# Gated window attention at decode: z turned by VectorE in column quarters, y and the gate among the queries, and wo's first piece loaded in two halves around the last values

## The chip, the cores and the metric

The kernel runs on one core of one Trainium2 chip. A time is the device time of one execution in microseconds; of several executions of a kernel the median is given. The profile is that of one further execution, taken by the hardware profiler; times inside it are counted from the start of its span. PE is TensorE's matrix array, PEld its weight load, DVE VectorE, ACT ScalarE, POOL GpSimd and SP SyncE, whose queue issues the large loads here.

## What is computed

One token for each of two sequences passes a layer norm, an attention over the last W = 4096 positions of a cache (32 query heads, 8 key and value heads, head size 128), and beside it a gated MLP; the attention's output is multiplied by silu of the MLP's output and added to x. All is float32.

```python
W = min(4096, max(256, Sk // 4))
xn = _layernorm(x)
q = (xn @ wq) as [B, 32, 1, 128]
k, v = k_cache[:, :, Sk - W:, :], v_cache[:, :, Sk - W:, :]   # repeated for 4 query heads each
p = softmax(q . k * 128 ** -0.5)
s = (p @ v) as [B, 1, 4096] @ wo                              # [4096, 512]
z = _gelu(xn @ w_in)                                          # [512, 1792]
z1, z2 = z[..., :896], _layernorm(z[..., 896:])
g = silu((z1 * (w_sp * z2 + b_sp)) @ w_out)                   # [896, 512]
out = x + s * g
```

The keys and values that are read are 2 x 8 x 4096 x 128 floats each, 33.6 MB; wq and wo are 8.4 MB each, w_in 3.7 MB and w_out 1.8 MB: 89.4 MB in all for a few matrix-vector products.

## The kernel before

**Loads.** Everything large is issued on SP's queue, in the order of the program. A ring of four buffers of 4 MB (`slot`, 32 KB in each of the 128 partitions) receives first w_in and the two halves of wq, then the keys and values, and last wo. The attention is done in eight units of two key and value heads of one sequence; `K:u` and `V:u` load the 4 MB of keys and the 4 MB of values of unit u. A load into a buffer waits, on SP, until the last reader of what was in it is done, and the loads behind it wait too.

**A unit.** VectorE turns the keys of a unit in eight pieces of 32 x 32 blocks (`T:u.q`), TensorE multiplies them with the queries in two halves (`shares`, `scores`, with a copy by ScalarE, `keep`, between), VectorE takes the maximum (`rowmax`, `mg`, `bias`), ScalarE the exponentials (`exp`), VectorE turns the probabilities (`probs_t`), TensorE multiplies them with the values in two halves (`pv:u.0`, `pv:u.1`), ScalarE scales the result (`evac`) and TensorE and VectorE collect it (`col`, `gather`). Units 0 to 3 belong to the first sequence, 4 to 7 to the second.

**wo.** The attention's 4096 outputs per sequence are split into three sets (`SETS`): set 0 from the units 0, 1, 4 and 5, set 1 from 2 and 6, set 2 from 3 and 7. `spread:i` and `oT:i` bring set i into the form of weights. `wo:0` loads the 4 MB of wo that belong to set 0 and `wo:1` the 2 MB of set 1 and the 2 MB of set 2, the latter in pieces of 4, 2, 1 and 1 blocks (a block is 256 KB). `X`, `Y` and `U` are the multiplications of set 0, of set 1 and of the first four blocks of set 2, two blocks in a step, accumulated over the four 32-column strips of the array in `part`; `parts:0` copies `part` to SBUF, `pz:0` sums its four strips into `so`, and `Z:n` adds the last three pieces of set 2 to `so`, in steps of one column quarter for each strip. Two operations of VectorE and a store to `out` end the program.

**Order.** All engines but POOL run in program order. From `K:0` on, that order is the text `ORDER` (lines 27 to 52), read from left to right; before that it is the order of the code. The change touches the code of lines 236 to 354 (the MLP and the queries), the text of `ORDER`, and the functions `load_wo`, `wo_early`, `wo_last` and `add_parts` (lines 518 to 563).

**The front part.** `z` (lines 236 to 248) multiplies xn with w_in, one bank for each quarter of the columns, with the four parts of the sum over 512 left apart in the four strips; the copy to SBUF is followed by 14 multiplications of z with a selection of rows (`zT_ps`), which sum the strips and turn the result. The gelu, the layer norm and `hT` follow on VectorE, with `queries(0)` to `queries(3)` (q = xn wq, one for each quarter of the sum) put between them on TensorE; then come `y` (hT w_out), the placing of the queries (`qs`, `qx`, `xm`, `qa`, `place_queries`) and `y_sum`; the gate is computed by the step `silu:0` in unit 0's work.

Each line of the trace is put down to line 65, the helper `InOrder`, so the tiles' names tell the operations apart.

Of the kernel before, what the change touches and what calls it, by code (L numbers as in the profile page):

```python
# [24 lines left out]


ORDER = """
K:0 K:1 V:0 T:0.0 q:0 T:0.1 T:0.2 T:0.3 shares:0.0 T:0.4 T:0.5 T:0.6 keep:0.0 scores:0.0 T:0.7 shares:0.1 keep:0.1
scores:0.1 rowmax:0.0
K:2 V:1 T:1.0 T:1.1 T:1.2 rowmax:0.1 mg:0 shmax:0 T:1.3 silu:0 bias:0 shares:1.0 T:1.4 exp:0.0 probs_t:0.0 T:1.5 T:1.6  # L30
exp:0.1 keep:1.0 pv:0.0 lsum:0 shsum:0 scores:1.0 T:1.7 shares:1.1 probs_t:0.1 pv:0.1 weights:0 keep:1.1 scores:1.1
evac:0 col:0 rowmax:1.0
K:3 V:2 T:2.0 T:2.1 T:2.2 rowmax:1.1 mg:1 shmax:1 T:2.3 bias:1 shares:2.0 T:2.4 exp:1.0 probs_t:1.0 T:2.5 T:2.6 exp:1.1
# [10 lines left out]
scores:5.1 evac:4 col:4 rowmax:5.0  # L44
K:7 V:6 T:6.0 rowmax:5.1 mg:5 T:6.1 T:6.2 shmax:5 bias:5 T:6.3 exp:5.0 T:6.4 exp:5.1 T:6.5 probs_t:5.0 shares:6.0
keep:6.0 lsum:5 shsum:5 scores:6.0 probs_t:5.1 T:6.6 T:6.7 rowmax:6.0 pv:5.0 weights:5 shares:6.1 keep:6.1 pv:5.1
V:7 T:7.0 wo:0 scores:6.1 rowmax:6.1 T:7.1 T:7.2 mg:6 T:7.3 shmax:6 bias:6 T:7.4 evac:5 col:5 exp:6.0 exp:6.1 T:7.5
probs_t:6.0 T:7.6 T:7.7 wo:1 lsum:6 shares:7.0 keep:7.0 pv:6.0 scores:7.0 shares:7.1 rowmax:7.0 keep:7.1 shsum:6
scores:7.1 probs_t:6.1 weights:6 rowmax:7.1 mg:7 pv:6.1 evac:6 shmax:7 gather:5 col:6 bias:7 exp:7.0 gather:6 exp:7.1
probs_t:7.0 spread:0 probs_t:7.1 lsum:7 spread:1 pv:7.0 shsum:7 oT:0 weights:7 pv:7.1 X:0.6 X:0.0 oT:1 X:0.2 X:0.4  # L50
evac:7 X:0.3 col:7 X:0.7 gather:7 spread:2 X:0.5 Y:0.1 Y:0.0 Y:0.3 X:0.1 Y:0.2 oT:2 U:0.0 U:0.1 parts:0 Z:0 pz:0 Z:1 Z:2
"""


# [16 lines left out]
def kernel(  # L71
# [14 lines left out]
    pe, dve, act, sp = (InOrder(tc, e) for e in (nc.tensor, nc.vector, nc.scalar, nc.sync))  # L86
    B, _, D = x.shape
# [39 lines left out]
    for a in range(0, KT, 2):  # L127
        t = slot(f"wq{a}", 2, HQ * DH)
# [30 lines left out]
    xnT = cst.tile([P, KT, 32], F32, tag="xnT", name="xnT")  # L159
# [3 lines left out]
    hT = cst.tile([P, FT, 32], F32, tag="hT", name="hT")  # L163
# [6 lines left out]
    rowm = cst.tile([P, 32], F32, tag="rowm", name="rowm")  # L170
# [24 lines left out]
    pt = bank("xnT_ps", KT, B)  # L195
# [30 lines left out]
    for nj in (8, 16):  # L226
# [3 lines left out]
        at = cst.tile([P, nx], F32, tag=f"at{nj}", name=f"at{nj}")  # L230
# [2 lines left out]

    assert KT == G
    z = kts.tile([P, F], F32, tag="kts", name="z")
    for n in range(G):
        pz = bank(f"z{n}", 512)[:, :FC]
        for k in range(KT):  # L240
            pe.matmul(
                pz[32 * k : 32 * k + 32, :], xnT[:, k, :], win[:, k, n * FC : (n + 1) * FC],
                start=True, stop=True,
            )
        if n % 2:
            dve.tensor_copy(z[:, n * FC : (n + 1) * FC], pz)
        else:
            act.activation(z[:, n * FC : (n + 1) * FC], pz, AF.Copy)
    wb_ps = ps.tile([P, 512], F32, tag="mo", name="wb_ps")[:, :2]
    pe.matmul(wb_ps, ones[0:1, :], wb1, start=True, stop=True)  # L250
    wb = cst.tile([P, 2], F32, tag="wb", name="wb")
    dve.tensor_copy(wb, wb_ps)
    pt = bank("zT_ps", 2, FT, B)
    zv = z.rearrange("b (h p j) -> b h j p", h=2, j=FT)
    for h in range(2):
        for j in range(FT):
            pe.matmul(pt[:, h, j, :], zv[:, h, j, :], rowm[:, :B], start=True, stop=True)


    assert HKV == NR * G  # L260
    pq = [ps.tile([P, 512], F32, tag=f"s{r}", name=f"q_ps{r}") for r in range(NR)]
# [1 line left out]
    def queries(k):  # L263
        for r in range(NR):
            for g in range(G):
                c = (r * G + g) * 512
                pe.matmul(
                    pq[r][32 * g : 32 * g + 32, :], xnT[:, k, :], wqt[k][:, c : c + 512],
                    start=(k == 0), stop=(k == KT - 1),
                )  # L270

    queries(0)
    zT = cst.tile([P, 2, FT, B], F32, tag="zT", name="zT")
    dve.tensor_copy(zT, pt)
    u = cst.tile([P, 2, FT, B], F32, tag="u", name="u")
# [17 lines left out]

    per_b = [[0, FT], [1, B]]
    mean_over_rows(mean, z2, "mean_ps")
    queries(1)
    dve.tensor_scalar_mul(mean, mean, 1.0 / FH)
    dve.tensor_sub(z2, z2, free_ap(mean, 0, per_b))
    dve.tensor_mul(w2, z2, z2)
# [3 lines left out]
    dve.tensor_mul(z2, z2, free_ap(mean, 0, per_b))  # L303
    dve.tensor_scalar(z2, z2, wb[:, 0:1], wb[:, 1:2], op0=ALU.mult, op1=ALU.add)
    dve.tensor_mul(hT[:, :, 0 : 16 * B : 16], z1, z2)
    queries(2)
    queries(3)

    HC = REP * G
    y = bank("y", D)
    for j in range(FT):
        g = j % G
        pe.matmul(y[32 * g : 32 * g + 32, :], hT[:, j, :], wout[:, j, :], start=(j < G), stop=(j >= FT - G))
    qs = kts.tile([P, NR, 512], F32, tag="kts", name="qs")
    qx = kts.tile([P, NR, HC, 32], F32, tag="kts", name="qx")
    for r in range(NR):
# [3 lines left out]
    for b in range(B):  # L322
# [1 line left out]
            xm[:, b], free_ap(qx, b, [[32 * HC, NR], [0, G], [32, HC]]), free_ap(grpm, 0, [[0, NR], [1, G], [0, HC]]),  # L324
            op=ALU.mult,
        )
    yp = sb.tile([P, D], F32, tag="o", name="yp", bufs=1)
    act.activation(yp, y, AF.Copy)
    qa = bank("qa", NP, G, REP)
    pe.matmul(  # L330
        qa.rearrange("p n c i -> p (n c i)"), same.rearrange("p g c -> p (g c)"),
        xm.rearrange("p b r g (i c) -> p (b r g) c i", c=G), start=True, stop=True,
    )

    y = bank("y_sum", DC)
    for g in range(G):
        pe.matmul(y[32 * g : 32 * g + 32, :], rowm, yp[:, g * DC : (g + 1) * DC], start=True, stop=True)
    ys = cst.tile([P, DC], F32, tag="ys", name="ys")
    act.activation(ys, y, AF.Copy)
# [7 lines left out]
    gate = cst.tile([P, DC], F32, tag="gate", name="gate")

    def silu():
        dve.tensor_scalar(gate, ys, -1.0, 80.0, op0=ALU.mult, op1=ALU.min)  # L350
        act.activation(gate, gate, AF.Exp)
        dve.tensor_scalar_add(gate, gate, 1.0)
        dve.reciprocal(gate, gate)
        dve.tensor_mul(gate, gate, ys)

# [9 lines left out]
    sets = {}  # L365
# [105 lines left out]
    col = {}  # L471
# [43 lines left out]
        wo_s.append(wo[r0:r1, :].rearrange("(p j) d -> p j d", j=nj))  # L515
    blocks = []

    def load_wo(n):
        t = slot(f"wo{n}", 16, D)
        a = 0  # L520
        for i in ((0,), (1, 2))[n]:
            for j, n in (((0, 16),), ((0, 8),), ((0, 4), (4, 2), (6, 1), (7, 1)))[i]:
                sp.dma_start(t[:, a : a + n, :], wo_s[i][:, j : j + n, :])
                blocks.append((t[:, a : a + n, :], sets[f"oT{i}"][1], j))
                a += n

    EARLY = 28
    done = 0
# [1 line left out]
    def wo_early(n, at):  # L530
        nonlocal done
        if done == 0:
            part.append(ps.tile([P, 512], F32, tag="s0", name="part"))
        t, oT, j = blocks[n]
        for a in range(at, at + 2):
            g = done % G
            pe.matmul(
                part[0][32 * g : 32 * g + 32, :], oT[:, j + a, :], t[:, a, :], start=(done < G), stop=(done >= EARLY - G)
            )
            done += 1  # L540
# [5 lines left out]
        act.activation(parts[0], part[0], AF.Copy)  # L546

    def wo_last(n):
        if n == 0:
            so.append(bank("so", DC))  # L550
        t, oT, j = blocks[3 + n]
        for a in range(t.shape[1]):
            for g in range(G):
                pe.matmul(
                    so[0][32 * g : 32 * g + 32, :], oT[:, j + a, :], t[:, a, g * DC : (g + 1) * DC],
                    start=(n == 0 and a == 0), stop=(j + a == oT.shape[1] - 1),
                )

    def add_parts():
        for g in range(G):  # L560
            pe.matmul(
                so[0][32 * g : 32 * g + 32, :], rowm, parts[0][:, g * DC : (g + 1) * DC], start=False, stop=False
            )

    parts, so = [], []
# [79 lines left out]
```

## Time and profile before

| | |
|---|---|
| median of 3 executions | 217.01 us (216.76, 217.04, 217.01) |
| the profiled execution's own time | 217.29 us |
| its span | 215.5 us |
| mean granted TensorE clock | 0.825 |
| busy: PE, DVE, ACT, POOL | 143.2, 126.7, 51.6, 4.5 us |
| read from HBM | 89.40 MB, 415 GB/s over the span |

The profiled execution spends 217.29 - 215.5 = 1.79 us outside the span, and is 0.28 us above the median. A busy time is the sum over an engine's instructions, with overlapping ones counted once; it says nothing of what the end waits for. In the lists of instructions a row gives the start, the duration, the engine, the operation with the tiles that it writes and reads, how many instructions are put together, and in brackets the idle time of the engine before them with what ended it. In the rows of windows the number behind an engine's name is its busy time in that stretch, and the last three are the granted clock of TensorE, the busy share of the DMA engines, and the data rate.

### The profile page before, as it was taken

The numbers are of one execution on the slowest core, as the hardware profiler recorded it, in microseconds if no ns is written. First come the engines' busy times: TensorE is split into PE (matmuls) and PEld (weight loads), VectorE is DVE, ScalarE is ACT, GpSimd is POOL, SyncE is SP. The second block draws the span as 40 slices with busy tenths as digits, with TensorE's granted clock in tenths as the row PEclk, the third lists the DMA queues.
The fourth block names the chain that finished last, engine by engine and source line by source line (L and its number), as shares of the span: only waits on it lengthen the run. The fifth ranks groups of instructions, "written<-read, shape, count | busy, mean of one in ns | idle before, by whom it ended". The sixth has DMA issues, their size and how long they took to land.

```text
span 215.5 us, 2332 instructions
## 1 busy us (share of the span) xinstructions
PE 143.2 (66%) x900; PEld 48.1 (22%) x900; DVE 126.7 (59%) x218; ACT 51.6 (24%) x129; POOL 4.5 (2%) x17
## 2 busy tenths in 40 slices
PE   0179796833854966964991795389259917987793
PEld 0117622111120221222220231123112201232231
DVE  2611213169899799649928972993698099636011
ACT  5011103300116036033330602142051206142201
POOL 8000000000000000000000000000000000000000
PEclk9999569665998896796697599669755997996999
DMA  7999999999999999999999999999999999999990
GB/s 246 432 443 444 398 429 465 414 458 414 456 408 447 420 426 444 426 443 426 450 420 450 408 441 420 426 450 426 447 415 456 401 456 414 447 426 417 420 374 22
DMA packets 3930, 89.54 MB, mean 416 GB/s; under 512 B 446, under 2 KB 462, under 8 KB 848
## 3 DMA queue, kind: packets, MB, share of 16 engines
q1 hardware_dynamic: 3900, 89.40, 96.8%
q8 instruction: 7, 0.11, 0.2%
q14 instruction: 3, 0.02, 0.0%
q10 hardware_dynamic: 20, 0.01, 0.0%
HBM read 89.40 MB, written 0.00 MB: 415 GB/s over the span
## 4 chain that ended last, share of the span: by engine, by line
DMA 63%; PE 23%; DVE 8%; ACT 3%; issue 1%; ACTq 0%
DMA v<-in_A_v_cache_dram 42%; DMA k<-in_A_k_cache_dram 16%; PE acc L65 10%; DMA win<-in_B_w_in_dram 5%; PE sh L65 5%; DVE kts L65 4%; PE part L65 4%; PE s L65 3%; DVE pT L65 1%; ACT p L65 1%; ACT o L65 1%; DVE gate L65 1%; PE mo L65 1%; ACT ss L65 1%; DVE qb L65 1%
## 5 line engine op out<-in xcount | busy, mean ns | idle before, releaser
L65 DVE STREAM_TRANSPOSE kts<-k 128x1024 f32<-128x1024 f32 x64 | 75.6, 1218 | 29.5 <-DMA k<-in_A_k_cache_dram 29.5
L65 PE MATMUL sh<-kts,qb 128*32 128x512 f32 x256 | 41.6, 775 | 13.2 <-DVE kts L65 9.3
L65 PE MATMUL acc<-v,pT 128*32 128x512 f32 x256 | 37.4, 707 | 8.8 <-DVE pT L65 4.4
L65 ACT ACTIVATE p<-s,nb 128x512 f32<-128x512 f32 x32 | 22.5, 733 | 36.2 <-DVE nb L65 36.2
L65 ACT ACTIVATE ss<-sh 128x512 f32<-128x512 f32 x16 | 9.6, 599 | 59.1 <-PE sh L65 59.1
L65 DVE STREAM_TRANSPOSE pT<-p 128x1024 f32<-128x1024 f32 x16 | 19.6, 1225 | 2.3 <-ACT p L65 2.1
L65 PE MATMUL s<-ss,sums 128*128 128x512 f32 x32 | 18.8, 671 | 2.3 <-ACT ss L65 2.3
L65 PE MATMUL mo<-mg,joint 128*128 128x16 f32 x16 | 4.0, 327 | 23.4 <-DVE mg L65 23.4
L65 PEld LDWEIGHTS acc<-v,pT 128*32 128x32 f32 x256 | 10.5, 145 | 35.1 <-issue 27.0
L65 PEld LDWEIGHTS sh<-kts,qb 128*32 128x32 f32 x256 | 8.8, 126 | 34.2 <-issue 28.8
L65 DVE TENSOR_REDUCE m<-s 128x1 f32<-128x512 f32 x16 | 10.7, 671 | 4.2 <-PE s L65 4.2
L65 PE MATMUL q_ps<-wq,xnT 128*32 128x512 f32 x64 | 10.5, 784 | 3.5 <-DMA wq<-in_A_wq_dram 3.5
L65 ACT ACTIVATE o<-acc,wd 128x128 f32<-128x128 f32 x32 | 9.1, 368 | 15.0 <-PE acc L65 15.0
L65 PEld LDWEIGHTS mo<-mg,joint 128*128 128x128 f32 x16 | 3.2, 250 | 27.2 <-DVE mg L65 24.4
L65 PE MATMUL z<-win,xnT 128*32 128x448 f32 x32 | 5.6, 869 | 4.7 <-DMA win<-in_B_w_in_dram 4.7
L65 PE MATMUL part<-wo,oT 128*32 128x512 f32 x56 | 7.7, 596 | 1.4 <-ACT o L65 1.4
L65 PEld LDWEIGHTS s<-ss,sums 128*128 128x128 f32 x32 | 5.0, 197 | 10.3 <-issue 7.7
L65 PE MATMUL zT_ps<-rowm,z 128*128 128x2 f32 x28 | 6.6, 370 | 0.0
L65 PEld LDWEIGHTS zT_ps<-rowm,z 128*128 128x128 f32 x28 | 6.5, 325 | 0.0
L65 ACT ACTIVATION_READ_ACCUMULATOR p<-s,nb 128x1 f32 x32 | 6.5, 203 | 0.0
L65 ACT ACT_TABLE_LOAD x4 | 5.1, 1283 | 2.6 <-POOL hT L164 2.6
L65 DVE COPY z<-z 128x448 f32<-128x448 f32 x2 | 1.3, 626 | 7.5 <-PE z L65 7.5
(111 smaller groups left out, 68.4 us busy)
## 6 DMA issues: line engine op xcount, KB each, us to landing
k<-in_A_k_cache_dram SPq DMA_DIRECT2D x8, 4096.0 KB, 27.4
v<-in_A_v_cache_dram SPq DMA_DIRECT2D x8, 4096.0 KB, 29.8
wq<-in_A_wq_dram SPq DMA_DIRECT2D x1, 4096.0 KB, 24.5
wq<-in_A_wq_dram SPq DMA_DIRECT2D x2, 2048.0 KB
wo<-in_A_wo_dram SPq DMA_DIRECT2D x1, 4096.0 KB, 30.4
win<-in_B_w_in_dram SPq DMA_DIRECT2D x1, 3584.0 KB, 11.5
wo<-in_A_wo_dram SPq DMA_DIRECT2D x1, 2048.0 KB
wout<-in_B_w_out_dram SPq DMA_DIRECT2D x1, 1792.0 KB, 15.3
```

What stands on the lines that cost most here:

```text
L65: return self.tc.keep_in_program_order(call(*args, **kwargs))
```

## The change

z now goes into one bank: the strip g of the array holds the g-th quarter of the columns of both halves of z, and the four parts of the sum are added up in the bank. One copy by ScalarE and one 32 x 32 turn by VectorE give z in the form in which the gelu needs it; the 14 multiplications `zT_ps` are gone. `queries(0)` and `queries(1)` come behind the whole layer norm, then `y`, `queries(2)`, `y_sum` with the gate, and `queries(3)`. The step `silu:0` is gone and `q:0` stands before `T:0.0`.

wo's set 0 is loaded in two halves, `wo:0.0` before `V:7` and `wo:0.1` behind it. The first half takes the ring's buffer of K:6 and V:7 that of V:5, where before V:7 took that of K:6 and wo that of V:5. Set 1 is `wo:1.0`, set 2 comes in pieces of 4, 3 and 1 blocks (`wo:2.0` to `wo:2.2`). The steps on the first half (`X:0.0` to `X:0.3`) stand between the probabilities of unit 7, those on the second half (`X:1.0` to `X:1.3`) behind `pv:7.1`, around `col:7` and `spread:2`; `Y`, `U`, `parts:0` follow, then `pz:0`, `Z:0` and `Z:1`, where before `Z:0` stood ahead of `pz:0`. `part` takes a buffer of `acc` in place of `s0`.

```diff
-K:0 K:1 V:0 T:0.0 q:0 T:0.1 T:0.2 T:0.3 shares:0.0 T:0.4 T:0.5 T:0.6 keep:0.0 scores:0.0 T:0.7 shares:0.1 keep:0.1
+K:0 K:1 V:0 q:0 T:0.0 T:0.1 T:0.2 T:0.3 shares:0.0 T:0.4 T:0.5 T:0.6 keep:0.0 scores:0.0 T:0.7 shares:0.1 keep:0.1
...
-V:7 T:7.0 wo:0 scores:6.1 rowmax:6.1 T:7.1 T:7.2 mg:6 T:7.3 shmax:6 bias:6 T:7.4 evac:5 col:5 exp:6.0 exp:6.1 T:7.5
-probs_t:6.0 T:7.6 T:7.7 wo:1 lsum:6 shares:7.0 keep:7.0 pv:6.0 scores:7.0 shares:7.1 rowmax:7.0 keep:7.1 shsum:6
-scores:7.1 probs_t:6.1 weights:6 rowmax:7.1 mg:7 pv:6.1 evac:6 shmax:7 gather:5 col:6 bias:7 exp:7.0 gather:6 exp:7.1
-probs_t:7.0 spread:0 probs_t:7.1 lsum:7 spread:1 pv:7.0 shsum:7 oT:0 weights:7 pv:7.1 X:0.6 X:0.0 oT:1 X:0.2 X:0.4
-evac:7 X:0.3 col:7 X:0.7 gather:7 spread:2 X:0.5 Y:0.1 Y:0.0 Y:0.3 X:0.1 Y:0.2 oT:2 U:0.0 U:0.1 parts:0 Z:0 pz:0 Z:1 Z:2
+wo:0.0 V:7 wo:0.1 T:7.0 scores:6.1 rowmax:6.1 T:7.1 T:7.2 mg:6 T:7.3 shmax:6 bias:6 T:7.4 evac:5 col:5 exp:6.0 exp:6.1
+T:7.5 gather:5 probs_t:6.0 T:7.6 T:7.7 wo:1.0 wo:2.0 wo:2.1 wo:2.2 lsum:6 shares:7.0 keep:7.0 spread:0 pv:6.0 scores:7.0
+shares:7.1 rowmax:7.0 keep:7.1 shsum:6 oT:0 scores:7.1 probs_t:6.1 weights:6 rowmax:7.1 mg:7 pv:6.1 evac:6 shmax:7 col:6
+bias:7 exp:7.0 gather:6 X:0.0 X:0.1 exp:7.1 probs_t:7.0 X:0.2 X:0.3 probs_t:7.1 lsum:7 spread:1 pv:7.0 shsum:7 weights:7
+pv:7.1 oT:1 X:1.0 evac:7 X:1.1 col:7 X:1.2 gather:7 spread:2 X:1.3 oT:2 Y:0.0 Y:0.1 Y:0.2 Y:0.3 U:0.0 U:0.1 parts:0 pz:0
+Z:0 Z:1
...
-    z = kts.tile([P, F], F32, tag="kts", name="z")
-    for n in range(G):
-        pz = bank(f"z{n}", 512)[:, :FC]
-        for k in range(KT):
+    pz = bank("z", 2, FH // G)
+    for k in range(KT):
+        for g in range(G):
             pe.matmul(
-                pz[32 * k : 32 * k + 32, :], xnT[:, k, :], win[:, k, n * FC : (n + 1) * FC],
-                start=True, stop=True,
+                pz[32 * g : 32 * g + 32], xnT[:, k, :],
+                win[:, k].rearrange("p (h g c) -> p h g c", h=2, g=G)[:, :, g, :],
+                start=(k == 0), stop=(k == KT - 1),
             )
...
+    zs = kts.tile([P, 2, 2, FT, 32], F32, tag="kts", name="zs")
+    act.activation(zs[:, 0], pz.rearrange("p h (i j) -> p h j i", j=FT), AF.Copy)
+    dve.transpose(zs[:, 1].rearrange("p h j i -> p (h j i)"), zs[:, 0].rearrange("p h j i -> p (h j i)"))
+    pt = zs[:, 1, :, :, :B]
...
-    pt = bank("zT_ps", 2, FT, B)
-    zv = z.rearrange("b (h p j) -> b h j p", h=2, j=FT)
-    for h in range(2):
-        for j in range(FT):
-            pe.matmul(pt[:, h, j, :], zv[:, h, j, :], rowm[:, :B], start=True, stop=True)
...
     dve.tensor_mul(hT[:, :, 0 : 16 * B : 16], z1, z2)
-    queries(2)
-    queries(3)
...
+    queries(0)
+    queries(1)
     y = bank("y", D)
...
+    yp = sb.tile([P, D], F32, tag="o", name="yp", bufs=1)
+    act.activation(yp, y, AF.Copy)
+    queries(2)
+    y = bank("y_sum", DC)
...
+    act.activation(gate, gate, AF.Exp)
+    dve.tensor_scalar_add(gate, gate, 1.0)
+    dve.reciprocal(gate, gate)
+    dve.tensor_mul(gate, gate, ys)
+    queries(3)
...
-    def load_wo(n):
-        t = slot(f"wo{n}", 16, D)
-        a = 0
-        for i in ((0,), (1, 2))[n]:
-            for j, n in (((0, 16),), ((0, 8),), ((0, 4), (4, 2), (6, 1), (7, 1)))[i]:
-                sp.dma_start(t[:, a : a + n, :], wo_s[i][:, j : j + n, :])
...
+    PIECES = (((0, 8), (8, 8)), ((0, 8),), ((0, 4), (4, 3), (7, 1)))
+    wo_t = {}
+
+    def load_wo(i, n):
+        if i < 2 and n == 0:
+            wo_t[i] = slot(f"wo{i}", 16, D)
+        t, at = (wo_t[i], 0) if i < 2 else (wo_t[1], 8)
+        j, count = PIECES[i][n]
+        sp.dma_start(t[:, at + j : at + j + count, :], wo_s[i][:, j : j + count, :])
...
-            part.append(ps.tile([P, 512], F32, tag="s0", name="part"))
+            part.append(ps.tile([P, 512], F32, tag="acc", name="part", bufs=2))
...
     def wo_last(n):
-        if n == 0:
-            so.append(bank("so", DC))
-        t, oT, j = blocks[3 + n]
+        t, oT, j = blocks[4 + n]
...
-                    start=(n == 0 and a == 0), stop=(j + a == oT.shape[1] - 1),
+                    start=False, stop=(j + a == oT.shape[1] - 1),
...
     def add_parts():
+        so.append(bank("so", DC))
         for g in range(G):
             pe.matmul(
-                so[0][32 * g : 32 * g + 32, :], rowm, parts[0][:, g * DC : (g + 1) * DC], start=False, stop=False
+                so[0][32 * g : 32 * g + 32, :], rowm, parts[0][:, g * DC : (g + 1) * DC], start=True, stop=False
             )
```

More of the change, by code (lines that the diff above doesn't have):

```diff
@@ L27 @@
 ORDER = """
-K:0 K:1 V:0 T:0.0 q:0 T:0.1 T:0.2 T:0.3 shares:0.0 T:0.4 T:0.5 T:0.6 keep:0.0 scores:0.0 T:0.7 shares:0.1 keep:0.1
+K:0 K:1 V:0 q:0 T:0.0 T:0.1 T:0.2 T:0.3 shares:0.0 T:0.4 T:0.5 T:0.6 keep:0.0 scores:0.0 T:0.7 shares:0.1 keep:0.1
 scores:0.1 rowmax:0.0
-K:2 V:1 T:1.0 T:1.1 T:1.2 rowmax:0.1 mg:0 shmax:0 T:1.3 silu:0 bias:0 shares:1.0 T:1.4 exp:0.0 probs_t:0.0 T:1.5 T:1.6
+K:2 V:1 T:1.0 T:1.1 T:1.2 rowmax:0.1 mg:0 shmax:0 T:1.3 bias:0 shares:1.0 T:1.4 exp:0.0 probs_t:0.0 T:1.5 T:1.6
 exp:0.1 keep:1.0 pv:0.0 lsum:0 shsum:0 scores:1.0 T:1.7 shares:1.1 probs_t:0.1 pv:0.1 weights:0 keep:1.1 scores:1.1
@@ L232 @@
         perms[nj] = to, at
-    assert KT == G
-    z = kts.tile([P, F], F32, tag="kts", name="z")
-    for n in range(G):
-        pz = bank(f"z{n}", 512)[:, :FC]
-        for k in range(KT):
+    assert KT == G and FT * 32 == FH // G
+    pz = bank("z", 2, FH // G)
+    for k in range(KT):
+        for g in range(G):
             pe.matmul(
-                pz[32 * k : 32 * k + 32, :], xnT[:, k, :], win[:, k, n * FC : (n + 1) * FC],
-                start=True, stop=True,
-            )
[L245 to L248, printed above, removed]
+                pz[32 * g : 32 * g + 32], xnT[:, k, :],
+                win[:, k].rearrange("p (h g c) -> p h g c", h=2, g=G)[:, :, g, :],
+                start=(k == 0), stop=(k == KT - 1),
+            )
+    zs = kts.tile([P, 2, 2, FT, 32], F32, tag="kts", name="zs")
+    act.activation(zs[:, 0], pz.rearrange("p h (i j) -> p h j i", j=FT), AF.Copy)
+    dve.transpose(zs[:, 1].rearrange("p h j i -> p (h j i)"), zs[:, 0].rearrange("p h j i -> p (h j i)"))
+    pt = zs[:, 1, :, :, :B]
     wb_ps = ps.tile([P, 512], F32, tag="mo", name="wb_ps")[:, :2]
@@ L270, in queries @@
                 )
-    queries(0)
     zT = cst.tile([P, 2, FT, B], F32, tag="zT", name="zT")
@@ L295 @@
     mean_over_rows(mean, z2, "mean_ps")
-    queries(1)
     dve.tensor_scalar_mul(mean, mean, 1.0 / FH)
@@ L305 @@
     dve.tensor_mul(hT[:, :, 0 : 16 * B : 16], z1, z2)
-    queries(2)
-    queries(3)
-    HC = REP * G
+    queries(0)
+    queries(1)
     y = bank("y", D)
@@ L315 @@
         pe.matmul(y[32 * g : 32 * g + 32, :], hT[:, j, :], wout[:, j, :], start=(j < G), stop=(j >= FT - G))
+    yp = sb.tile([P, D], F32, tag="o", name="yp", bufs=1)
+    act.activation(yp, y, AF.Copy)
+    queries(2)
+    y = bank("y_sum", DC)
+    for g in range(G):
+        pe.matmul(y[32 * g : 32 * g + 32, :], rowm, yp[:, g * DC : (g + 1) * DC], start=True, stop=True)
+    ys = cst.tile([P, DC], F32, tag="ys", name="ys")
+    act.activation(ys, y, AF.Copy)
+    gate = cst.tile([P, DC], F32, tag="gate", name="gate")
+    dve.tensor_scalar(gate, ys, -1.0, 80.0, op0=ALU.mult, op1=ALU.min)
+    act.activation(gate, gate, AF.Exp)
[3 more added lines that the diff above has]
+    queries(3)
+    HC = REP * G
     qs = kts.tile([P, NR, 512], F32, tag="kts", name="qs")
@@ L326 @@
         )
-    yp = sb.tile([P, D], F32, tag="o", name="yp", bufs=1)
-    act.activation(yp, y, AF.Copy)
     qa = bank("qa", NP, G, REP)
@@ L333 @@
     )
[L335 to L339, printed above, removed]
     def place_queries():
@@ L345, in place_queries @@
         )
[L347 to L354, printed above, removed]
     JH = UJ // 2
@@ L516 @@
     blocks = []
-    def load_wo(n):
-        t = slot(f"wo{n}", 16, D)
-        a = 0
-        for i in ((0,), (1, 2))[n]:
-            for j, n in (((0, 16),), ((0, 8),), ((0, 4), (4, 2), (6, 1), (7, 1)))[i]:
-                sp.dma_start(t[:, a : a + n, :], wo_s[i][:, j : j + n, :])
-                blocks.append((t[:, a : a + n, :], sets[f"oT{i}"][1], j))
-                a += n
+    PIECES = (((0, 8), (8, 8)), ((0, 8),), ((0, 4), (4, 3), (7, 1)))
[6 more added lines that the diff above has]
+        sp.dma_start(t[:, at + j : at + j + count, :], wo_s[i][:, j : j + count, :])
+        blocks.append((t[:, at + j : at + j + count, :], sets[f"oT{i}"][1], j))
     EARLY = 28
@@ L574, in step @@
             place_queries()
-        elif name == "silu":
-            silu()
         elif name == "K":
@@ L581, in step @@
         elif name == "wo":
-            load_wo(u)
+            load_wo(u, a[0])
         elif name == "spread":
@@ L587, in step @@
         elif name == "X":
-            wo_early(0, 2 * a[0])
+            wo_early(u, 2 * a[0])
         elif name == "Y":
-            wo_early(1, 2 * a[0])
+            wo_early(2, 2 * a[0])
         elif name == "U":
-            wo_early(2, 2 * a[0])
+            wo_early(3, 2 * a[0])
         elif name == "Z":
```

## The prediction

> **What bounds the kernel now.** I read the page first, for the busy shares and the chain, then the chain in order of time, and then instructions and windows at both ends.
>
> ```profile
> span 215.5 us, 2332 instructions
> ...
> DMA  7999999999999999999999999999999999999990
> ...
> q8 instruction: 7, 0.11, 0.2%
> ...
> L65 DVE STREAM_TRANSPOSE kts<-k 128x1024 f32<-128x1024 f32 x64 | 75.6, 1218 | 29.5 <-DMA k<-in_A_k_cache_dram 29.5
> ```
>
> The DMA engines are busy in every slice but the last, while VectorE, next after TensorE, idles 29.5 us ahead of the keys' turns: the loads set the pace. That holds only while SP issues early enough. The chain, and SP's issues with the time to landing (last column of the rows with KB), show that it does:
>
> ```profile
> 12.23 33.92 DMA k<-in_A_k_cache_dram
> ...
> 150.21 32.33 DMA v<-in_A_v_cache_dram
> ...
> 206.95 3.64 PE part L65 x28
> ```
>
> ```profile
> 165.36 0.54 SPq L65 DMA_DIRECT2D v<-in_A_v_cache_dram  x1
> ...
> 171.62 0.34 SPq L65 DMA_DIRECT2D wo<-in_A_wo_dram  x1
> ...
> 184.22 0.33 SPq L65 DMA_DIRECT2D wo<-in_A_wo_dram  x1
> ...
> 186.02 0.43 SPq L65 DMA_DIRECT2D wo<-in_A_wo_dram  x1
> ...
> wo<-in_A_wo_dram SPq DMA_DIRECT2D x1, 4096.0 KB, 30.4
> ...
> wo<-in_A_wo_dram SPq DMA_DIRECT2D x1, 256.0 KB, 25.7
> ```
>
> V:6 lands at 150.21 + 32.33 = 182.54, wo's 4 MB at 171.62 + 30.4 = 202.0. Between them lie V:7's 4 MB and wo's: 19.5 us for 8 MB, so 2.43 us per MB. The last 256 KB land at 186.02 + 25.7 = 211.7. All issues from V:7 on are made 25 us or more before their data land, so when SP issues is not what counts here.
>
> The end of the program, on three engines:
>
> ```profile
> 202.11 2.34 PE L65 MATMUL part<-wo,oT 128*32 128x512 f32 x18 [1.36 <-ACT o L65]
> ...
> 205.87 4.71 PE L65 MATMUL part<-wo,oT 128*32 128x512 f32 x32
> ...
> 210.62 0.64 PE L65 MATMUL so<-wo,oT 128*32 128x128 f32 x16
> 210.68 0.60 ACT L65 ACTIVATE parts<-part 128x512 f32<-128x512 f32 x1 [8.67 <-PE part L65]
> ...
> 211.33 0.43 PE L65 MATMUL so<-parts,rowm 128*32 128x128 f32 x8
> ...
> 211.57 0.65 PE L65 MATMUL so<-wo,oT 128*32 128x128 f32 x16
> 212.28 0.29 DVE L65 TENSOR_TENSOR res<-so,gate 128x128 f32<-128x128 f32 x1 [5.71 <-PE so L65]
> ```
>
> X starts at 202.11, just after the 4 MB land (the bracket names ScalarE, which had ended by then). Y starts at 206.95, 2 MB or 4.87 us later; U's megabyte lands at 209.3. Z:0 at 210.62 comes with 512 KB more (1.2 us), and Z:2, the second half of the last row, with the last piece. TensorE follows the data from piece to piece, and its last pass ends 0.5 us behind the last landing. The bytes are the same after the change, so little but this end can be won or lost.
>
> **The change, part by part.**
>
> The front part:
>
> ```profile
> 12.35 5.56 PE L65 MATMUL z<-win,xnT 128*32 128x448 f32 x32 [4.73 <-DMA win<-in_B_w_in_dram]
> ...
> 14.12 0.54 ACT L65 ACTIVATE z<-z 128x448 f32<-128x448 f32 x1 [8.55 <-PE z L65]
> ...
> 18.15 6.60 PE L65 MATMUL zT_ps<-rowm,z 128*128 128x2 f32 x28
> ...
> 24.78 0.19 DVE L65 COPY zT<-zT_ps 128x28 f32<-128x28 f32 x1 [6.12 <-PE zT_ps L65]
> ...
> 26.18 3.64 PE L65 MATMUL q_ps<-wq,xnT 128*32 128x512 f32 x16 [1.43 <-DMA wq<-in_A_wq_dram]
> ...
> 36.69 2.79 PE L65 MATMUL q_ps<-wq,xnT 128*32 128x512 f32 x16 [2.09 <-DMA wq<-in_A_wq_dram]
> ...
> 42.15 1.30 DVE L65 STREAM_TRANSPOSE qx<-qs 128x512 f32<-128x512 f32 x2 [5.68 <-PE y L65]
> ```
>
> The multiplications of z keep their number and width: 5.56 us, to 17.9. The 28 passes of `zT_ps`, 6.60 us, go; one copy (0.54) and one turn of 448 columns (0.65, half of the `qx` row) come. zT is there at about 19.4 in place of 25.0. But `queries(0)` starts at 26.18 because wq lands then, and `queries(3)` at 36.69 for the same reason, so the 5.6 us become a wait for wq. `y` now runs between landings, the `qx` turns lose their 5.68 us wait for it, and the queries are placed some 2 us sooner; unit 0's keys land at 12.23 + 33.92 = 46.15 all the same. Moving the gate frees VectorE in unit 0, in time that it then spends waiting for keys. V:0's issue may come up to a microsecond sooner or later; two loads are in flight. Worth zero on the path; the cover is the transfer of wq and the keys, and without it the part would be worth up to those 5.6 us.
>
> The loads of wo: six issues as before, the same bytes. On SP, wo:0.0 takes V:7's place at 165.36 and V:7 the one at 171.62, wo:0.1 right behind it, wo:1.0 at 184.22 as before; what stands behind each wait has 12 us or more of data queued ahead of it. At 2.43 us per MB, wo:0.0 lands at 187.4, V:7 at 197.2 (before 192.3), wo:0.1 at 202.0, set 1 at 206.9, set 2 at 209.3, 211.1 and 211.7. Splitting the 4 MB: zero, as the wo pieces of 2 MB to 256 KB together took 211.7 - 202.0 = 9.7 us, the pace of a whole 4 MB.
>
> The values: V:7 is 4.9 us later.
>
> ```profile
> 195.29 3.27 PE L65 MATMUL acc<-v,pT 128*32 128x512 f32 x16 [1.38 <-DVE pT L65]
> 198.48 0.38 PE L65 MATMUL mo<-l,heads 128*128 128x1 f32 x2
> 198.80 1.95 PE L65 MATMUL acc<-v,pT 128*32 128x512 f32 x16
> ```
>
> `pv:7.0` moves from 195.29 to 197.3, and `pv:7.1` ends at 201.5 at the rate of the third row. ScalarE's scaling, `col`, `gather`, `spread:2` and `oT:2` need about 3 us more, to 204.8; U needs them at 209.4. Cost zero, cover 4.6 us. The passes on wo:0.0 run at 193 to 195, in a gap of TensorE.
>
> The end: before, four passes of X stood among Y (28 passes in 3.64 us). Now Y is 16 passes: 1.95 us from 206.95, to 208.9, and TensorE is idle when U's data land. A pass takes 0.60 and four start together, so four more cost (1.95 - 0.60) / 3 = 0.45; U's eight take 1.05, from 209.4 to 210.45, where `part` was done at 210.59: 0.14 gained. But now all four last blocks stand behind `pz:0`. Before, 24 passes followed there, 211.33 to 212.22; now 40 do. Sixteen more cost between 0.40 (16 passes in 0.65, of which 0.27 is the last one alone) and 0.48 (eight from 211.33 to 211.57); I take 0.44. Sum with the clock unchanged: -0.14 + 0.44 = +0.30.
>
> **The clock.** The new order leaves TensorE little to do between `X:1.3` and Y, about 204.8 to 206.9. What such a stretch does, in windows of the grid on which the granted clock changes (PE busy first, granted clock third from the end):
>
> ```profile
> 174.15:177.56 3.41, 0.44 (x6) 0.42 (x10) 3.41 (x6) 0.00 (x0) 0.00 (x0) 1.00 0.93 404
> 177.56:180.97 3.41, 3.09 (x24) 0.70 (x21) 3.38 (x6) 2.40 (x7) 0.00 (x0) 0.50 1.05 452
> ...
> 191.21:194.63 3.42, 1.72 (x18) 1.05 (x14) 1.34 (x4) 3.19 (x11) 0.00 (x0) 1.00 0.95 412
> 194.63:198.04 3.41, 2.75 (x16) 0.60 (x16) 2.25 (x5) 0.70 (x3) 0.00 (x0) 0.50 0.96 413
> 198.04:201.45 3.41, 2.71 (x26) 0.82 (x18) 0.79 (x4) 0.58 (x3) 0.00 (x0) 1.00 0.95 408
> 201.45:204.87 3.42, 2.76 (x32) 1.33 (x32) 0.00 (x0) 0.56 (x3) 0.00 (x0) 1.00 0.96 410
> 204.87:208.28 3.41, 3.00 (x28) 0.98 (x24) 0.78 (x3) 0.00 (x0) 0.00 (x0) 1.00 0.99 413
> ```
>
> 0.44 and 1.72 us of work were followed by half the clock, 2.7 and more by the full one. Before, the last windows hold 2.76 and 3.00. In the new order the window from 204.87 would hold Y's first 1.33 us, and one from 203.4 some 1.4 us of X: both below 1.72. Then Y, or its end and U, run at half rate. Y's four rounds would last 3.6 for 1.8 us, less the 0.65 that Y can be late before U waits for it: +1.15. By the row of 3.27 us for 1.95 it is 1.32 - 0.65 = +0.67. I take +0.95, nearer the first, as Y lies wholly in the slow window where it begins late enough. Sum: 0.30 + 0.95 = +1.25.
>
> [...]
>
> **The rivals.**
> - *The clock drops at the end* (my forecast): 217.01 + 1.25 = 218.3. For it: the windows. Against it: the bound between 1.72 and 2.75 is known from few rows.
> - *The clock stays*: 217.01 + 0.30 = 217.3, no measurable change. For it: two stretches of 16 passes on either side of a pause of 2 us can each fill their window; against it the low sums above.
> - *Faster, by when the DMA engines end.*
>
> ```profile
> 209.00:210.00 1.00, 1.00 (x12) 0.30 (x8) 0.00 (x0) 0.00 (x0) 0.00 (x0) 1.00 0.72 274
> 210.00:211.00 1.00, 0.96 (x23) 0.41 (x16) 0.00 (x0) 0.32 (x1) 0.00 (x0) 1.00 0.32 121
> 211.00:212.00 1.00, 0.93 (x35) 0.53 (x24) 0.00 (x0) 0.27 (x1) 0.00 (x0) 1.00 0.04 16
> ```
>
> The engines do not end together: the shares fall from 0.72 to 0.04. The seven packets of instructions take 0.2% of 16 engines' span, 0.002 x 16 x 215.5 / 7 = 1.0 us each, on the engine that they meet. With 56 TensorE instructions fewer they come at other moments. If one misses the engine that ends last, all landings come up to 1.0 us sooner: 217.01 + 0.30 - 1.0 = 216.3. It decides from 0.7 us on, where it outweighs the 0.30 and the bound of 0.2%. Against it: their number hardly changes.
> - *The values come too late*: only if `oT:2` is more than 4.6 us late, with both halves of `pv:7` at half clock (2 x 1.32) and more behind them: up to 1.5 us beyond the forecast, 219.8.
>
> **How the numbers follow.** Of this kernel about 0.2% (0.43 us) can be told from no change: the three executions span 0.28. Clock drop 0.45, clock stays 0.31, DMA engines end sooner 0.14, values late 0.05, and 0.05 for a tail that costs somewhat more than 0.43 without the drop. Faster is 0.14, within 0.2% 0.31, slower 0.55. The likeliest time is 218.3 (217.6 to 218.6 for that case alone). The range of 216.8 to 218.6 leaves out most of the third case and the late values, and holds the second. The sum is made against the profiled execution, 217.29, which lies 0.28 above the median; I add it to the median.
>
> **What would show it.** Right: `zT` at about 19.4 and `queries(0)` still at 26.2; V:7's use at 197.3, with its DMA wait; Y from 206.95; a window at 0.50 that covers Y or U; 40 passes of `so` behind `parts`; `res` at 213.5 in place of 212.28. Wrong: the clock at 1.00 from 202 on with `res` at 212.6; or landings of wo earlier than 202.0 and 206.9; or `queries(0)` waiting for the MLP, not for wq.

## The result: slower by 0.17%, all of it behind the last landing

The changed kernel takes 217.21 us, the median of 21 executions (217.04 to 217.55), the kernel before, on the same chips, 216.87 (216.64 to 217.08). The ratio is 1.0017, with a 95% interval of 1.0011 to 1.0023: 0.34 us slower, clear of noise and just inside the 0.2% that I had set as the bound. Forecast were 218.3 us and a drop of TensorE's clock at the end; the measured time is that of the rival in which the clock stays, 217.3.

The page of the profiled execution of the changed kernel (217.04 us, span 215.3):

```profile
span 215.3 us, 2273 instructions
...
DMA  7999999999999999999999999999999999999990
...
L66 DVE STREAM_TRANSPOSE kts<-k 128x1024 f32<-128x1024 f32 x64 | 75.5, 1218 | 34.1 <-DMA k<-in_A_k_cache_dram 34.1
```

The loads set the pace as before; VectorE waits 34.1 us for keys in place of 29.5, which is where most of the time that the front part saves has gone. The front part itself, in the order of time:

```profile
11.97 6.05 PE L66 MATMUL z<-win,xnT 128*32 128x448 f32 x32 [4.10 <-DMA win<-in_B_w_in_dram]
...
18.66 0.65 DVE L66 STREAM_TRANSPOSE zs<-zs 128x448 f32<-128x448 f32 x1 [8.57 <-ACT zs L66]
...
19.34 0.18 DVE L66 COPY zT<-zs 128x28 f32<-128x28 f32 x1
...
25.81 6.39 PE L66 MATMUL q_ps<-wq,xnT 128*32 128x512 f32 x32 [2.08 <-DMA wq<-in_A_wq_dram]
```

The copy that makes zT starts at 19.34 in place of 24.78, and the queries still begin when wq lands. TensorE at the end:

```profile
196.66 1.95 PE L66 MATMUL acc<-v,pT 128*32 128x512 f32 x16 [1.92 <-DMA v<-in_A_v_cache_dram]
...
201.47 1.07 PE L66 MATMUL part<-wo,oT 128*32 128x512 f32 x8 [0.66 <-DMA wo<-in_A_wo_dram]
...
206.41 1.92 PE L66 MATMUL part<-wo,oT 128*32 128x512 f32 x16 [1.46 <-DMA wo<-in_A_wo_dram]
208.84 1.07 PE L66 MATMUL part<-wo,oT 128*32 128x512 f32 x8 [0.51 <-DMA wo<-in_A_wo_dram]
210.67 0.42 PE L66 MATMUL so<-parts,rowm 128*32 128x128 f32 x8 [0.77 <-ACT parts L66]
210.92 1.06 PE L66 MATMUL so<-wo,oT 128*32 128x128 f32 x32
```

Every group on wo now waits for its data, U included, and the 32 passes of Z run in one piece behind `pz:0`. The last piece's issue with its time to landing, and the first of the two closing operations:

```profile
185.22 0.43 SPq L66 DMA_DIRECT2D wo<-in_A_wo_dram  x1
```

```profile
DMA to landing us min/median/max: 25.8/25.9/26.0
```

```profile
212.04 0.29 DVE L66 TENSOR_TENSOR res<-so,gate 128x128 f32<-128x128 f32 x1 [7.44 <-PE so L66]
```

The last piece lands at 185.22 + 26.0 = 211.2, and `res` starts 0.86 us behind it (211.18 with one more digit); before it was 212.28 - 211.75 = 0.53. The difference is 0.33 us, the measured loss. The last landing is only the mark from which this is counted. The chain of work that ended last in the changed kernel does not pass through it:

```profile
184.28 24.43 DMA wo<-in_A_wo_dram
...
208.84 1.10 PE part L66 x8
...
210.03 0.60 ACT parts L66
...
210.67 1.34 PE so L66 x40
```

It runs from the landing of U's megabyte at 208.71 through U's eight passes and ScalarE's copy into the 40 passes; the last piece lands while these are running. (That all landings of this execution are half a microsecond sooner than in the one shown before is not the change: `win`, which nothing precedes, already lands 0.38 sooner, and that execution of the kernel before, at 217.29, lay above all 21 of the comparison.)

The grid on which the clock changes, in the same columns as before:

```profile
198.65:202.06 3.41, 2.75 (x26) 0.88 (x26) 0.79 (x4) 1.13 (x4) 0.00 (x0) 1.00 0.99 423
202.06:205.47 3.41, 2.89 (x26) 0.90 (x18) 0.78 (x3) 0.01 (x1) 0.00 (x0) 1.00 0.97 416
205.47:208.89 3.42, 1.97 (x20) 0.58 (x24) 0.00 (x0) 0.00 (x0) 0.00 (x0) 1.00 0.98 411
208.89:212.30 3.41, 2.31 (x48) 1.14 (x48) 0.26 (x1) 0.60 (x1) 0.00 (x0) 1.00 0.31 119
```

The clock is 1.00 to the end.

### The profile page after: what moved, and what is told of

Same layout as the page of the kernel before. It is cut to its first block, busy times and chain, and to the rows that moved or that the text cites. A ratio compares the mean times of both kernels' runs of the same rounds, so it can differ in the third digit from the quotient of the medians.

```text
span 215.3 us, 2273 instructions
## 1 busy us (share of the span) xinstructions
PE 135.4 (63%) x872; PEld 42.5 (20%) x872; DVE 126.1 (59%) x217; ACT 51.4 (24%) x128; POOL 4.5 (2%) x17
## 4 chain that ended last, share of the span: by engine, by line
DMA 69%; DVE 22%; PE 3%; ACT 3%; issue 1%; SPq 0%; ACTq 0%
DMA k<-in_A_k_cache_dram 53%; DVE kts L66 18%; DMA wo<-in_A_wo_dram 11%; DMA win<-in_B_w_in_dram 5%; DVE pT L66 2%; ACT p L66 2%; PE sh L66 2%; DVE m L66 1%; PE so L66 1%; DVE nb L66 1%; PE s L66 1%; PE part L66 1%; ACT parts L66 0%; ACT ss L66 0%; DVE res L66 0%
## 5 line engine op out<-in xcount | busy, mean ns | idle before, releaser
L66 DVE STREAM_TRANSPOSE kts<-k 128x1024 f32<-128x1024 f32 x64 | 75.5, 1218 | 34.1 <-DMA k<-in_A_k_cache_dram 34.1
L66 PE MATMUL sh<-kts,qb 128*32 128x512 f32 x256 | 44.7, 825 | 16.1 <-DVE kts L66 12.4
L66 PE MATMUL acc<-v,pT 128*32 128x512 f32 x256 | 34.1, 649 | 4.9 <-DMA v<-in_A_v_cache_dram 4.9
L66 PE MATMUL q_ps<-wq,xnT 128*32 128x512 f32 x64 | 11.0, 784 | 3.2 <-DMA wq<-in_A_wq_dram 3.2
L66 PE MATMUL z<-win,xnT 128*32 128x448 f32 x32 | 6.1, 936 | 4.1 <-DMA win<-in_B_w_in_dram 4.1
L66 DVE STREAM_TRANSPOSE zs<-zs 128x448 f32<-128x448 f32 x1 | 0.6, 645 | 8.6 <-ACT zs L66 8.6
L66 PE MATMUL xnT_ps<-ident,xn 2*128 2x2 f32 x4 | 0.6, 252 | 7.3 <-DVE xn L66 7.3
```

Of the source, the lines that this page charges most:

```text
L66: return self.tc.keep_in_program_order(call(*args, **kwargs))
```

## The experiments

The first theory was that the order at the end alone costs the 0.34 us: Z:0 behind `pz:0`. Its rivals were the clock, the later values, and a front part that is not neutral.

**Z:0 put back ahead of pz:0 in the changed kernel (z_first).** Whichever of the two comes first opens the bank `so`, here and in the kernels below.

```diff
-... U:0.0 U:0.1 parts:0 pz:0 Z:0 Z:1
+... U:0.0 U:0.1 parts:0 Z:0 pz:0 Z:1
```

> The changed kernel with Z:0 put back ahead of pz:0, all else as changed. Theory (the order at the end): the 0.34 us that the change cost are the 16 passes of Z:0 that stand behind the copy of part and pz:0; ahead of them they run while ScalarE copies. The end is then set by the last landing again, as in the kernel before: ratio 1.000, 216.9 us, res 0.5 us behind the last landing of wo. Rival (the clock drops between X and Y in some executions): nothing of that changes, ratio stays at 1.0017. Rival (V:7 behind wo's first half delays the data): also 1.0017.

Measured: 217.31 us, ratio 1.0015 (1.0006 to 1.0023). The theory, in this form, falls. TensorE's instructions at the end of this kernel:

```profile
209.10 1.06 PE L66 MATMUL part<-wo,oT 128*32 128x512 f32 x8 [0.51 <-DMA wo<-in_A_wo_dram]
210.94 0.86 PE L66 MATMUL so<-wo,oT 128*32 128x128 f32 x24 [0.78 <-DMA wo<-in_A_wo_dram]
211.59 0.43 PE L66 MATMUL so<-parts,rowm 128*32 128x128 f32 x8
211.81 0.43 PE L66 MATMUL so<-wo,oT 128*32 128x128 f32 x8
```

Z:0 now waits for its own data. The piece of three blocks lands 0.6 us before the last one, at 210.8, when ScalarE has all but finished the copy (210.28 to 210.88), so Z:0 runs beside none of it; the 24 passes and then `pz:0` and Z:1 stand behind that landing. It is the same 40 passes in another order: `res` is again 0.86 us behind the last landing. Before, Z:0 had two blocks; it starts on them at 210.62, 1.13 us before the last landing (211.75), and runs while ScalarE copies (210.68 to 211.28).

**Z:0 put behind pz:0 in the kernel before (z_late).**

```diff
-... U:0.0 U:0.1 parts:0 Z:0 pz:0 Z:1 Z:2
+... U:0.0 U:0.1 parts:0 pz:0 Z:0 Z:1 Z:2
```

> The kernel before with Z:0 put behind pz:0, all else as before. Theory (the order at the end): 16 more passes of so behind the copy, 0.40 to 0.48 us; part is not done sooner here, so nothing is taken off: 217.3 us, ratio 1.0020. Rivals (clock, landing of V:7): the kernel before with its own clock and its own loads, ratio 1.000.

Measured: 217.47 us, ratio 1.0023 (1.0015 to 1.0032); 0.94 us between the last landing and `res`, 0.41 more than before. So the order alone costs this much where the pieces are small enough to profit from the old one.

**The front part alone (front_only), and the wo part alone (wo_only).** The first is the kernel before with lines 236 to 354 as changed, `q:0` ahead of `T:0.0` and no `silu:0`; the second has all the rest of the change on the old front part.

> The kernel before with only the front part of the change: z in column quarters turned by VectorE, y and the gate among the queries, q:0 ahead of T:0.0. Theory: the 5.6 us that zT comes sooner become a wait for wq; queries(0) starts at the landing of wq; ratio 1.000 (within 0.0005). Rival (the front part helps, and hides a larger loss at the end): ratio under 0.999. Rival (the front part costs): ratio 1.001 to 1.002.

> The kernel before with only the part of the change that concerns wo and the end (loads in halves, order of X, Y, U, pz and Z). Theory: all of the change, ratio 1.0017, 217.2 us. Rival (the front part costs): ratio 1.000.

Measured: 216.97 us, ratio 1.0003 (0.9993 to 1.0012), for the front part, and 217.28 us, ratio 1.0018 (1.0009 to 1.0027), for the wo part. The loss is the wo part's; the front part shows no effect, within 0.1% either way.

The theory that was left: the pieces and the order together. Two kernels separate them.

**Pieces of 2, 1 and 1 blocks in the changed kernel, with Z:0 ahead of pz:0 (pieces_z_first) and without (pieces_only).**

```diff
-    PIECES = (((0, 8), (8, 8)), ((0, 8),), ((0, 4), (4, 3), (7, 1)))
+    PIECES = (((0, 8), (8, 8)), ((0, 8),), ((0, 4), (4, 2), (6, 1), (7, 1)))
...
-... wo:2.0 wo:2.1 wo:2.2 ... parts:0 pz:0 Z:0 Z:1
+... wo:2.0 wo:2.1 wo:2.2 wo:2.3 ... parts:0 Z:0 pz:0 Z:1 Z:2     (pieces_z_first)
+... wo:2.0 wo:2.1 wo:2.2 wo:2.3 ... parts:0 pz:0 Z:0 Z:1 Z:2     (pieces_only)
```

> The changed kernel with the last half of wo's set 2 again in pieces of 2, 1 and 1 blocks (before: 3 and 1) and Z:0 ahead of pz:0. Theory (16 passes more behind the last gap, from the pieces and the order together): Z:0 starts at the landing of the 512 KB, runs while ScalarE copies part, Z:2 starts at the last landing: res 0.53 us behind it, ratio 1.000, 216.9 us. Rival (the rest of the wo part costs: V:7 later, X in two halves, the place of part): ratio stays near 1.0015.

> The changed kernel with the pieces of 2, 1 and 1 blocks alone, Z:0 to Z:2 behind pz:0. Theory: 40 passes still stand behind the copy of part, res 0.86 us behind the last landing, ratio 1.0017. Rival (only the 768 KB piece is to blame): ratio 1.000.

Measured: ratio 1.0000 (0.9991 to 1.0010) with both, 1.0017 (1.0007 to 1.0026) with the pieces alone. The end of the first, TensorE's rows with `res`, from the order of time:

```profile
210.26 0.65 PE L66 MATMUL so<-wo,oT 128*32 128x128 f32 x16 [0.17 <-DMA wo<-in_A_wo_dram]
210.85 0.43 PE L66 MATMUL so<-parts,rowm 128*32 128x128 f32 x8
211.09 0.78 PE L66 MATMUL so<-wo,oT 128*32 128x128 f32 x16
```

Z:0 runs from 210.26, beside the copy, and the last passes wait inside the last row for the final landing, 211.40 here; `res` follows at 211.94, 0.54 behind it, as before the change. With this, V:7's later place and wo's two halves are settled as well: they are in this kernel, and what they cost is nothing within 0.1%.

**The second half of X left out (no_x1).** The steps X:1.0 to X:1.3 are taken out of `ORDER` (and the count of early steps, `EARLY`, is lowered to match, here and in the next two kernels), so the pause that I had expected to cost the clock is almost empty.

> The changed kernel without X:1.0 to X:1.3 (the product with the second half of set 0 is left out of the sum; the load stays). TensorE then has only col:7 and spread:2 between the end of pv:7.1 (200.8) and Y (206.4). If a pause of this kind halves the clock of Y and U: a window at 0.50 that covers them, Y's 16 passes last 3.3 us for 1.92, and the time rises by 0.7 to 1.15 us over the changed kernel, to 218.0 or more, in most executions. If the clock keeps through such a pause, 217.2 as in the changed kernel.

Measured: 218.61 us (218.05 to 219.41), ratio 1.0069 (1.0048 to 1.0091): at least 0.84 us above the changed kernel's median in each execution. Its windows, and the row of Y and U:

```profile
200.60:204.02 3.42, 1.51 (x18) 0.46 (x10) 0.44 (x2) 1.14 (x4) 0.00 (x0) 1.00 0.99 426
204.02:207.43 3.41, 0.58 (x4) 0.23 (x8) 0.34 (x2) 0.00 (x0) 0.00 (x0) 0.50 0.96 405
207.43:210.84 3.41, 3.41 (x20) 0.91 (x16) 0.00 (x0) 0.00 (x0) 0.00 (x0) 0.50 0.70 288
```

```profile
206.84 4.74 PE L66 MATMUL part<-wo,oT 128*32 128x512 f32 x24 [3.01 <-DMA wo<-in_A_wo_dram]
```

The drop of the forecast exists: the granted clock is 0.50 from 204.02 to 210.84, and Y and U take 4.74 us from Y's landing, where the changed kernel has U done 208.84 + 1.07 - 206.41 = 3.50 us behind it, 1.24 more. Between these two kernels it is the work that the second half of X does in the pause that keeps the clock: 1.00 to the end with it, 0.50 without.

**The pause filled with narrow multiplications (narrow_fill).** no_x1, with nine multiplications of 16 columns between `spread:2` and Y.

```diff
+    def fill():
+        t = ps.tile([P, 512], F32, tag="s1", name="fill")
+        for _ in range(9):
+            pe.matmul(t[:, :16], ident, x4[:, :16], start=True, stop=True)
```

> The kernel without X:1 (its product with the second half of set 0 is left out), with 9 narrow multiplications (18 passes of 16 columns, result unused) between spread:2 and Y, so that PE is shown busy for some 2 to 3 us of the pause while it streams almost nothing. If busy time holds the clock (as the prediction took it, bound between 1.72 and 2.75 us of a window): the clock stays and the time is that of the changed kernel, 217.2 us. If what counts is the columns streamed, the clock still halves: 218.0 us or more, as without the fill.

Measured: 218.69 us; five of six executions at 218.34 or more, one at 217.25. The profiled one:

```profile
203.90:207.32 3.42, 3.01 (x36) 2.49 (x32) 0.78 (x3) 0.00 (x0) 0.00 (x0) 1.00 1.00 425
207.32:210.73 3.41, 3.41 (x24) 0.81 (x16) 0.00 (x0) 0.00 (x0) 0.00 (x0) 0.50 0.75 309
```

3.01 us of PE busy in 36 passes, and half the clock in the next window. Of the 3.01 us the 18 passes of the fill make 2.13, and Y's first eight, which are wide, 0.48. Here 3.01 us of busy time did not hold the clock. The fill also holds up Y: by the distance between set 1's landing and the last one in no_x1 (206.84 and 211.62) and the last landing here (211.10), I estimate that Y could have started at 206.3 here, and it started at 206.84. So the 2.36 us behind the last landing in the table below are not the clock's alone.

**Half of X's second half left out (half_x1).** X:1.2 and X:1.3 are taken out of `ORDER`: eight wide passes in the pause.

> The changed kernel without X:1.2 and X:1.3 (these four blocks are left out of the sum): 8 wide passes in the pause in place of 16. If the changed kernel is near the bound, most executions lose the clock here: 218.0 us or more. If it is far from it, the time stays at 217.2 in nearly all.

Measured: 218.35 us, ratio 1.0083 (1.0055 to 1.0111), none under 218.21. By these times, half of the wide passes is too little in every execution. (The profiled one, 220.29 us, was granted 0.57 to 0.65 in the stretches read from 20 us on, 0.639 over its span; the mean of the other five is 0.81 to 0.84. It is no test of the pause, and that the other five lost the clock is read from their times alone.)

**x added inside the matrix product (x_in_so).** If only what stands behind the last landing counts, the add of x there is worth its 0.33 us. On the kernel before, x over the gate is formed in unit 0 and put into `so` while TensorE waits for Z:0's data; at the end one multiplication is left.

```diff
         dve.tensor_mul(gate, gate, ys)
+        dve.tensor_scalar_add(gate, gate, 1e-30)
+        dve.reciprocal(xg, gate)
+        dve.tensor_mul(xg, xg, x4)
...
             so.append(bank("so", DC))
+            pe.matmul(so[0], ident, xg, start=True, stop=False)
...
     dve.tensor_mul(res, so[0], gate)
-    dve.tensor_add(res, res, x4)
```

> The kernel before with x added inside the matrix product: x divided by the gate is computed in unit 0 and put into so by one multiplication with the identity ahead of Z:0, so that one multiplication by the gate is all that VectorE does at the end (the add of 0.33 us goes). Theory (what stands behind the last landing, and only that, sets the end): 0.33 us less, ratio 0.9985, 216.55 us. Rival (the store or something else fixed ends the program): ratio 1.000.

Measured: 216.64 us against 216.96, ratio 0.9983 (0.9973 to 0.9994): the one version that beats both kernels, though the small number 1e-30 that keeps the division defined is a weakness where the gate is that close to zero.

All kernels together; the last landing of wo and the start of `res` are those of each profiled execution:

| kernel | last landing | `res` starts | behind it | ratio |
|---|---|---|---|---|
| before | 211.75 | 212.28 | 0.53 | 1 |
| changed | 211.18 | 212.04 | 0.86 | 1.0017 |
| front_only | 211.41 | 211.94 | 0.53 | 1.0003 |
| wo_only | 211.21 | 212.07 | 0.86 | 1.0018 |
| z_first | 211.44 | 212.30 | 0.86 | 1.0015 |
| z_late | 211.24 | 212.18 | 0.94 | 1.0023 |
| pieces_only | 211.41 | 212.18 | 0.77 | 1.0017 |
| pieces_z_first | 211.40 | 211.94 | 0.54 | 1.0000 |
| no_x1 | 211.62 | 213.73 | 2.11 | 1.0069 |
| narrow_fill | 211.10 | 213.46 | 2.36 | 1.0077 |
| x_in_so | 211.07 | 211.61 | 0.54, and no add | 0.9983 |

The landings scatter by 0.7 us without regard to the kernel; the ratios go with the fourth column, with the add of x counted too for x_in_so.

## Why the prediction was right and wrong

- *What bounds the kernel: right.* The loads are the pace, and only the stretch behind the last landing moved the time.
- *The front part, zero: right.* zT's copy ends at 19.34 + 0.18 = 19.52 (forecast about 19.4), the queries are still at wq's landing, ratio 1.0003 alone. That the time fits so closely is in part luck: the multiplications of z took 6.05 us, not 5.56, and began 0.38 sooner.
- *The loads and the values, zero: right.* pieces_z_first, which has V:7's later place and wo's two halves, is at 1.0000.
- *The end with the clock unchanged, +0.30: right, with its parts.* U's eight passes took 1.07 (forecast 1.05), `part` was done 0.11 sooner against the last landing (forecast 0.14), the 40 passes behind the copy lasted from 210.67 to 211.98, 1.31 (forecast 1.33), and the sum came to 0.33 by the trace and 0.34 by the medians. What the working left open is that it has two causes, of which neither alone undoes it: with the three-block piece the old order helps nothing (z_first), and with small pieces the new order costs as much (pieces_only).
- *The clock, +0.95: wrong; this is the step that failed.* I took the bound from PE's busy time, between 1.72 and 2.75 us of a window, and put Y's window (1.33) and X's (1.4) below it. Both sides of that are wrong. The pause holds more work than I counted: 2.89 us in the profiled window, and 1.95 in that of pieces_z_first from 203.30, where I had put 1.4 from 203.4. And a window with 1.97 us, or 1.95 in pieces_z_first, kept the clock, while 3.01 us in narrow_fill, most of them narrow passes, lost it. The measure and the count of the work were wrong, not the mechanism: with X's second half gone the clock halves and costs 1.25 us (2.11 against 0.86 in the table), somewhat more than the 0.67 to 1.15 that I had priced.

```profile
203.30:206.71 3.41, 1.95 (x14) 0.60 (x14) 0.49 (x2) 0.00 (x0) 0.00 (x0) 1.00 0.95 402
206.71:210.13 3.42, 2.86 (x24) 0.52 (x19) 0.00 (x0) 0.00 (x0) 0.00 (x0) 1.00 0.90 362
```

  These are the windows of pieces_z_first over the same pause: 14 passes run in the first, twelve of them 512 columns wide. The profile of the kernel before already held rows against the bound, which the prediction does not show:

```profile
17.13:20.54 3.41, 3.41 (x21) 2.69 (x13) 0.69 (x2) 0.52 (x1) 0.00 (x0) 1.00 1.07 461
20.54:23.96 3.42, 3.42 (x17) 3.42 (x16) 0.00 (x0) 0.00 (x0) 0.00 (x0) 0.50 0.95 412
...
170.73:174.15 3.42, 1.86 (x10) 0.30 (x2) 1.24 (x2) 1.14 (x4) 0.00 (x0) 1.00 0.98 422
174.15:177.56 3.41, 0.44 (x6) 0.42 (x10) 3.41 (x6) 0.00 (x0) 0.00 (x0) 1.00 0.93 404
```

  PE is never idle in the first window, 2.39 us of it in passes of `zT_ps` that are two columns wide, and the clock halves (0.50 in the next); so busy time is not the measure. In the second pair 1.86 us of passes of 512 columns keep the clock (1.00 in the next), which alone would have put the bound between 1.72 and 1.86.
- *A drop in some executions only: not seen, but for narrow_fill.* In the profiles of the kernel before and of the changed one every change of the granted clock lies on a grid of 3.41 us, and the grid lies elsewhere in each profile: a window starts at 198.04 in the kernel before, at 198.65 in the changed one, at 200.60 in no_x1. In the changed kernel's 21 executions the highest lies 0.34 above the median, and in the 44 of the four other kernels with the whole second half of X none lies more than 0.4 above its own. By these times no share of executions lost the clock there, and with eight wide passes fewer (half_x1) none kept it. In narrow_fill one of six, by its time of 217.25, kept it; the place of the grid may have decided there, which no trace shows. The last section gives a count that fits all three.
- *Faster, by when the DMA engines end: did not happen.* Landings scatter by 0.7 us, of the 1.0 that I had allowed, but not with the change.

## What to carry to other kernels

Where loads fill the whole time, count the passes behind the last landing, and look for each of them when its own data land and what it waits for besides: the size of the last pieces and the order of the steps have to fit each other, and a reading that changes only one of them finds nothing (here 1.0015 and 1.0017, and 1.0000 with both). Do not price a clock drop from the busy time of a window, of which 3.01 us lost the clock here and 1.95 kept it; compare with windows whose instructions are of the same width and run on as many strips at once. A forecast with one well-priced small term and one large doubtful one should lead with the first unless the second's bound has rows close on both sides of it.

## What the runs showed of the hardware that I had not expected

In narrow_fill a window of 3.41 us with 3.01 us of PE busy, all but 0.48 in passes of 128 columns or fewer, was followed by half the clock (0.50); in pieces_z_first one with 1.95 us, most of it in passes of 512, was followed by the full one (1.00). In no_x1's window from 200.60 to 204.02, with 1.51 us busy, the longest gap between passes is 1.31 us, and the clock halved (0.50) at its end. front_only has another window of narrow passes, in the middle of the last units:

```profile
190.45:193.87 3.42, 2.20 (x22) 1.05 (x14) 0.85 (x4) 2.71 (x9) 0.00 (x0) 1.00 1.04 450
193.87:197.28 3.41, 2.26 (x12) 0.61 (x16) 2.73 (x5) 1.19 (x4) 0.00 (x0) 0.50 0.98 418
```

Of its 22 passes 14 are those of `mo`, `col` and `spread`, 128 columns or fewer; the others are the end of one group on the values. Its 2.20 us of busy time lost the clock, where 1.95 us of mostly wide passes kept it. But the sum of the columns does not sort the windows either, as two rows of the kernel before show:

```profile
34.20:37.61 3.41, 1.32 (x16) 0.32 (x16) 1.30 (x7) 0.71 (x2) 0.00 (x0) 1.00 1.18 500
37.61:41.02 3.41, 3.41 (x23) 0.82 (x18) 0.00 (x0) 1.19 (x2) 0.00 (x0) 0.50 0.98 423
```

The clock was lost (1.00, then 0.50) after 16 passes of 512 columns, twelve of them begun in the window, that ran four at a time. pieces_z_first kept it with twelve, eight of them begun in the window, of which those of X ran two at a time.

A count that sorts the windows of these traces, an estimate of mine, is the time in which columns stream on at least one strip. In the changed kernel the weights of the rounds of `sh`, 512 columns each, are loaded at 168.33, 168.76 and 169.20 at full clock, and at 178.41 and 179.26 at half. So I count 0.43 us per 512 columns from each pass's start (0.86 at half clock), leave out the rest of its duration, and count strips that run together once. In the traces of the kernel before and the changed one 70 windows begin at full clock. The 20 of them that half the clock followed hold at most 1.16 us; the 50 that kept it hold 1.31 or more. PE's busy time, in the same windows, goes up to 3.41 where the clock was lost and down to 1.67 where it was kept. Of the 44 windows at half clock the 20 behind which the full clock came back hold 2.58 us or more, the 24 others at most 2.45. Over all eleven traces without half_x1 the groups touch: of 385 windows at full clock the 102 that lost it hold at most 1.25 us, and the 283 that kept it 1.24 or more, but for one of 1.15; behind half clock the full one came back 102 times, from 2.57 us on, and did not 136 times, up to 2.56. These are figures of this case's windows; what the clock goes by, no run here shows.

By this count the emptiest stretch of 3.41 us from 196 us to the end of TensorE's work on wo holds 1.42 us in the changed kernel, wherever the grid lies. With the eight passes of X:1.2 and X:1.3 taken out of that trace, every place of the grid has a window of 1.22 or less, and in narrow_fill's trace all but a few places have one under 1.24. That would explain why, by their times, no execution of the first lost the clock, none of half_x1 kept it and one of narrow_fill did. It is an estimate that fits the windows; no experiment here was made to test it.
